# Transposing the second gate-gradient pair and the last filter group by transfers instead of TensorE

## The chip, the core and the metric

One program on one core of a Trainium2 chip. The core has TensorE (matmuls, weight loads), VectorE, ScalarE and GpSimd, a sequencer SP that issues most transfers, and 16 DMA engines that carry them. The metric is device time in microseconds: the median over executions, each compared with executions of the kernel before on the same chip.

## The reference

Forward and backward of one block. `q`, `k`, `v` are 2048 x 512 (sequence by channels); the filter `ssm_k` is 512 x 2048.

```
xn   = layernorm(q)
kv   = (causal 4-tap filter of k with shift_k) * v
y    = causal convolution of kv with ssm_k along the sequence, per channel + kv * ssm_D
s    = xn * y
z    = (sigmoid(xn @ w_gate) * (xn @ w_up)) @ w_down
out  = q + s * silu(z)
```

It returns `out` and the gradients, for a given `grad_out`, of q, k, v, shift_k, ssm_k, ssm_D, w_gate, w_up, w_down. In the backward pass the gradient of `z` (`dz`, 2048 x 512, the "gate gradient" here) is multiplied by the transposed `w_down`, and what comes of it by the transposed `w_gate` and `w_up`.

## The kernel before, in words

The sequence is cut into 16 tiles of 128 rows, taken as 8 pairs (`NP = 8`); the channels into four groups of 128 (`NG = 4`). Convolutions are FFTs of 4096 points, done as matmuls: `step1` multiplies 128x128 tables `Cf` with the 16 column blocks of a group, a 32x32 stream transpose on VectorE follows (`flip`), then `step2`, 32 small matmuls of 32x32 weights in two pairs of PSUM banks. `inv2` and `inv1` go back.

Streams that run side by side: `strG` computes the gated unit pair by pair (`gu_gen`: gate and up matmuls with 256 columns; `z_gen`: 11 matmuls with 512 columns for each tile). `strK` transforms the filter group by group: it loads `KT`, 128 channels x 2048 taps, transposes it into `KC` (16 blocks of 128x128, where block j takes every sixteenth tap), and does `step1` and `step2`. `strV` does the same for `kv`, `strX` multiplies the spectra. Then the backward pass: `zs_gen` computes `dz` of a pair and its transpose `dzT`, `dh_gen` multiplies it by `WdT` (44 matmuls of 256 columns for a pair), `x_gen` multiplies by `WgT` and `WuT` (11 matmuls of 512 columns with each, for each tile). At the end the weights' gradients (`dW`) and the convolution's backward (`frontC`, `backC`).

The pairs go backward in the order `ORD = [5, 6, 7, 4, 3, 2, 1, 0]`, so pair 6 is the second of this order. Of the 8 transposes `dzT` in the kernel before, those of the first two pairs are done by TensorE (8 transposes of 128x128 for a pair, with two copies out of PSUM), the other six by a transposing transfer from SBUF to SBUF. Of the four filter groups all are transposed by TensorE, 16 transposes and two copies of 1,024 columns each.

Nothing is issued in program order. The program is recorded as a list of numbered operations, and `ORDER` gives, written out, the order of the numbers for each engine: `tensor`, `vector`, `scalar`, `gpsimd`, `sync` (SP's transfers); `moves` orders the transfers among each other as the program is emitted. "25 15+1" means 25, 15, 16. Engines take their lists strictly in order. A copy out of PSUM (`evac`) may stand in the list of ScalarE or of VectorE. `BANKS` gives each PSUM tile its place. Every operation is recorded at one line of code (507), so rows of the trace are told apart by tiles, shapes and times; with 4,907 numbers in the tensor list and 4,907 matmuls in the trace, a number's place in time can be counted off.

Numbers that the prediction touches, as the kernel before has them: 3 is the load of columns 0 to 255 of `w_up` on ScalarE's queue, 119 and 127 start the gate and the up matmuls that use those columns for pair 0; 192 is a sigmoid. 1156 to 1163 and 1201 to 1208 are the transposes of the last filter group, 1164 and 1209 their copies, 1360 starts the `step1` matmuls of that group. 1095 is the copy of a `step1` tile of `strV`, 1014 and 1022 a `step2` of `strK`, 1165 to 1174 ten `z_gen` matmuls. 2351 to 2360 are the transposes and copies of pair 6; 2476 and 2482 the transposing loads of `w_gate` and `w_up` into `WgT` and `WuT`, 2265 a small load for `WuT`'s last 96 columns, 2297 a store of `out`; 2474 a load of `grad_out`. 2575 and 2546 start the two tiles of `x_gen` of the first pair, 2586 and 2557 their parts that use `WuT`; 2607, 2627, 2647 and 2655 are `dh_gen` of pair 6.

Of the kernel before, what the change touches and what calls it, by code (L numbers as in the profile page):

```python
# [9 lines left out]
ALU = mybir.AluOpType  # L10
# [13 lines left out]
NJ = 16  # L24
# [53 lines left out]
    """,  # L78
    "vector": """
# [552 lines left out]
def kernel_impl(ctx, tc, A_q, A_k, A_v, A_shift_k, A_ssm_k, A_ssm_D, B_x, B_w_gate, B_w_up, B_w_down,  # L632
# [24 lines left out]
    def ps(kind, shape, dt=f32):  # L657
        return nc.ps(kind, shape, dt)
# [870 lines left out]
```

## Time and profile before

| | before |
|---|---|
| median of 3 runs | 448.35 us (447.02 to 449.74) |
| the profiled execution | 445.85 us, span of the core 443.7 us |
| TensorE matmuls | 435.5 us, 98% of the span, 4,907 |
| TensorE weight loads | 303.8 us, 68% |
| VectorE | 409.3 us, 92%, 629 instructions |
| ScalarE | 279.8 us, 63%, 352 instructions |
| GpSimd | 20.9 us, 5% |
| transfers | 116.85 MB, mean 263 GB/s |

The span runs from the core's first instruction to its last; the profiled execution's own time lies 2.15 us above it. Shares are averages over stages; a matmul's end is modelled. PE is TensorE, PEld its weight loads, DVE VectorE, ACT ScalarE, SP the sequencer that issues transfers; a q behind the name (SPq, ACTq) is that engine's queue. "x16 | 1.2, 227" in a group means 16 instructions, 1.2 us busy together, 227 ns for one.

### The profile page before, as it was taken

Reading aid. Unit: us, or ns where it says so; the run is one execution under the profiler, and the core shown is the slowest. Engines: PE = TensorE matmul, PEld = TensorE weight load, DVE = VectorE, ACT = ScalarE, POOL = GpSimd, SP = SyncE. Lnnn points to the kernel's source line nnn. Section 1 sums busy time; section 2 is a strip of 40 time slices with the busy share of each in tenths; the row PEclk is TensorE's granted clock in tenths of the full one; section 3 lists DMA queues with packets and bytes.
Section 4 is the critical chain, followed back from the end, with each engine's and each line's share of the span. In section 5 each row is a group of like instructions: output and inputs, shape, how many; then the busy total and the mean of one; then the engine's idle time right before and its main releaser. Section 6 shows DMA issues by size and latency. Waiting matters only on the chain.

```text
span 443.7 us, 11573 instructions
## 1 busy us (share of the span) xinstructions
PE 435.5 (98%) x4907; PEld 303.8 (68%) x4907; DVE 409.3 (92%) x629; ACT 279.8 (63%) x352; POOL 20.9 (5%) x46
## 2 busy tenths in 40 slices
PE   7999999999999999999999999999999999999996
PEld 3886686767758678565656654444478888887885
DVE  8999899989988999999999987699889999999993
ACT  6998898888756688545283543534577745574422
POOL 8210110000000000000000000000000000000000
PEclk9999999999999999999999999999999999999999
DMA  7999998678398899999989999999999999999998
GB/s 245 297 349 282 294 315 264 167 273 305 116 312 261 247 222 222 284 322 308 363 236 324 289 216 282 279 241 186 281 258 215 267 267 219 231 249 262 266 258 260
DMA packets 196069, 116.85 MB, mean 263 GB/s; under 512 B 107386, under 2 KB 182706, under 8 KB 195890
## 3 DMA queue, kind: packets, MB, share of 16 engines
q1 hardware_dynamic: 186864, 111.49, 94.5%
q10 hardware_dynamic: 9154, 4.62, 3.5%
q8 instruction: 38, 0.62, 0.6%
q14 instruction: 13, 0.11, 0.1%
HBM read 43.87 MB, written 46.70 MB: 204 GB/s over the span
## 4 chain that ended last, share of the span: by engine, by line
PE 88%; DVE 6%; ACT 2%; DMA 1%; POOL 1%; issue 1%
PE psum L507 88%; DVE slab L507 6%; ACT slab L507 2%; POOL slab L507 1%; DMA slab<-in_A_q_dram 1%; DMA slab<-in_A_ssm_k_dram 1%
## 5 line engine op out<-in xcount | busy, mean ns | idle before, releaser
L507 PE MATMUL psum<-slab 128*128 128x256 bf16 (+5 forms) x4907 | 435.5, 299 | 4.0 <-DVE slab L507 3.2
L507 PEld LDWEIGHTS <-slab 128*128 128x128 bf16 (+2 forms) x4907 | 303.8, 96 | 135.6 <-issue 28.9
L507 ACT CAST slab<-psum 128x1024 bf16<-128x1024 f32 (+5 forms) x224 | 190.4, 892 | 119.5 <-PE psum L507 96.0
L507 DVE TENSOR_TENSOR slab<-slab 128x1024 bf16<-128x1024 bf16 (+4 forms) x302 | 240.2, 830 | 8.0 <-ACT slab L507 6.2
L507 ACT ACTIVATE slab<-slab 128x512 bf16<-128x512 bf16 (+5 forms) x61 | 50.9, 875 | 30.8 <-DVE slab L507 30.7
L507 DVE STREAM_TRANSPOSE slab<-slab 128x1024 f32<-128x1024 f32 x48 | 64.8, 1354 | 1.8 <-ACT slab L507 1.3
L507 DVE CAST slab<-psum 128x1024 bf16<-128x1024 f32 (+3 forms) x29 | 32.6, 1131 | 5.1 <-PE psum L507 4.3
L507 DVE TENSOR_TENSOR slab<-psum,slab 128x512 bf16<-128x512 f32 (+2 forms) x52 | 31.5, 609 | 5.9 <-ACT slab L507 3.8
L507 ACT ACTIVATE slab<-psum 128x512 bf16<-128x512 f32 (+1 forms) x48 | 27.6, 576 | 7.1 <-PE psum L507 6.8
L507 POOL MEMSET slab<- 128x128 bf16 (+3 forms) x10 | 4.5, 448 | 261.8 <-DVE slab L507 149.6
L507 POOL TENSOR_TENSOR slab<-slab 128x2 f32<-128x2 f32 (+3 forms) x11 | 11.0, 1000 | 97.3 <-DVE slab L507 97.2
L507 DVE SCALAR_TENSOR_TENSOR slab<-slab 128x2 f32<-128x2 f32 (+2 forms) x41 | 14.1, 359 | 1.5 <-POOL slab L507 1.2
L507 ACT ACT_TABLE_LOAD x10 | 12.8, 1283 | 1.9 <-issue 1.8
L507 DVE SCALAR_TENSOR_TENSOR slab<-psum,slab 128x512 bf16<-128x512 f32 x16 | 10.7, 684 | 1.9 <-PE psum L507 1.8
L507 DVE BATCH_NORM_STATS2 slab<-slab 128x6 f32<-128x512 bf16 x16 | 10.7, 678 | 1.0 <-DMA slab<-in_A_q_dram 1.0
L507 DVE STREAM_SHUFFLE slab<-slab 128x1024 f32<-128x1024 f32 x8 | 10.5, 1319 | 0.0
L507 ACT COPY slab<-psum 128x1024 bf16<-128x1024 bf16 (+2 forms) x9 | 7.4, 831 | 0.8 <-PE psum L507 0.8
L507 DVE TENSOR_SCALAR slab<-slab 128x512 bf16<-128x512 bf16 (+6 forms) x28 | 7.5, 284 | 0.2
L507 DVE COPY slab<-psum 128x512 bf16<-128x512 bf16 (+1 forms) x10 | 4.7, 492 | 0.1
L507 POOL TENSOR_SCALAR slab<-slab 128x1 f32<-128x1 f32 (+3 forms) x10 | 3.3, 335 | 0.4
L507 DVE MEMSET slab<- 32x192 uint32 (+3 forms) x10 | 1.6, 160 | 1.7 <-PEq L1513 0.9
L507 DVE BATCH_NORM_AGGREGATE slab<-slab 128x2 f32<-128x6 f32 x16 | 2.6, 167 | 0.1
(13 smaller groups left out, 8.4 us busy)
## 6 DMA issues: line engine op xcount, KB each, us to landing
slab<-KD SPq DMA_DIRECT2D x16, 512.0 KB, 5.3
hD<-slab SPq DMA_DIRECT2D x8, 704.0 KB, 6.1
duD<-slab SPq DMA_DIRECT2D x8, 704.0 KB, 5.4
dgD<-slab SPq DMA_DIRECT2D x8, 704.0 KB, 5.1
slab<-in_A_k_dram SPq DMA_DIRECT2D x4, 1024.0 KB, 7.6
KD<-slab SPq DMA_DIRECT2D x8, 512.0 KB, 5.5
VD<-slab SPq DMA_DIRECT2D x8, 512.0 KB, 5.5
out_dram<-slab SPq DMA_DIRECT2D x16, 256.0 KB, 4.1
```

The costliest lines, as they stand in the source:

```text
L507: getattr(getattr(self.nc, eng), meth)(*[place(v) for v in a], **{x: place(v) for x, v in k.items()})
```

## The change

Two transposes move from TensorE to transposing transfers on SP's queue.

In `strK`, the last group (`cg == 3`) no longer uses TensorE: `KT` is copied into `Q` with its taps reordered, so that block j is contiguous (one copy of 128x2048, which `ORDER` gives to ScalarE), and a transposing transfer writes `KC` from `Q`. 16 transposes and two copies of 1,024 columns go.

In `zs_gen`, TensorE transposes only the first pair of `ORD`; the second pair gets a transposing transfer as the later pairs have. 8 transposes and two copies of 512 columns go.

All lists of `ORDER` and `BANKS` are new. The program has 25 operations fewer, so numbers shift: below 1156 they stay; the copy into `Q` is 1156, the transposing transfer to `KC` 1193; from 1210 on a number falls by 16, the transfer of `dzT` of pair 6 is 2335, and from 2361 on a number falls by 25. So 2476 becomes 2451, 2482 becomes 2457, 2265 becomes 2249, 2297 becomes 2281, 2474 becomes 2449, and 2575, 2607, 2546, 2627 become 2550, 2582, 2521, 2602. Twenty copies out of PSUM change from VectorE to ScalarE and 21 from ScalarE to VectorE.

The diff, of `ORDER` only the lines that hold these places:

```diff
...
     "tensor": """
...
-        1210+15 968+7 1042+3 1033+7 1054+1 1087+7 1165+3 1004+7 1169+5 1022+7 1014+7 1056+8 1175 1106+7 1098+7 1238+15
...
-        2443+3 2277+3 2458+1 2272+3 2466+6 2460 2488+15 2351+3 2508+15 2356+3 2536+3 2528+7 2483+3 2627+15 2477+3
-        2607+15 2575+9 2546+10 2655+3 2647+7 2557+10 2702+3 2585+11 2746+15 2706+3 2766+15 2665+7 2794+3 2786+7
...
+        1087+7 1004+7 1157+9 1022+7 1014+7 1054+1 1167 1056+8 1106+7 1098+7 1230+7 1222+7 1287+7 753+7 769+7 745+7
...
+        2401+7 2393+7 2210+15 2418+3 2414+3 2157+15 2425+5 2437+3 2256+3 2261+3 2431+4 2441+6 2463+15 2483+15 2511+3
+        2503+7 2452+3 2550+3 2582+15 2458+3 2521+7 2602+15 2630+3 2622+7 2554+17 2529+13 2677+3 2721+15 2741+15 2769+3
...
     "scalar": """
-        1 68 60+1 66 65 67 249+1 69 327 251+1 307 3 279 112 62 192 410 438 541 363 362 586 596 560 135 477 524 686 385
...
+        1 68 60+1 65+2 249+1 327 69 307 251+1 279 112 62 192 3 410 438 541 363 362 586 560 596 135 524 477 686 220 384
...
+        674 985 966 1002 652+1 1041 976 1210 1050 1156 1095 1312 1030+1 1168 1065 1114+1 1238 778 1303 777 1342 1188+1
...
     "sync": """
...
-        1939 1936 1933 1759 1935 1942 1938 2062 1940 1934 1943 1963 2082 2019 2262 2267 2263 2298 2474 2265 2268 2323
-        2476 2297 2482 2738 2438 2324 2544 2701 2475 2545 2449 2737 1770 2743 2663 2606 1937 2739 2605 2664 2802 2868
...
+        365 937 386 709 506 708 722 655 675 938 617 399 936 707 1193 940 780 1066 793 743 917 1052 1154 1314 1410 1169
...
+        1925 1920 1743 1923 1767 1917 2046 1926 1922 2047 1924 1927 1947 1919 2066 2003 2246 2282 2251 2307 2252 2247
+        2451 2335 2281 2249 2457 2308 2449 2520 2676 2713 2413 2424 2712 2519 2450 2581 2718 2639 2638 2714 2580 1754
...
@@ -977,17 +977,23 @@
             if cg > 0:
                 nc.vector.tensor_tensor(KT[:, 0:1], KT[:, 0:1], Dcol_b[:, cg:cg + 1], ALU.add)
             KC = KC_r.next()
-            for jh in range(2):
-                pt = ps("tr", [8, 128], bf16)
-                for jj in range(8):
-                    nc.tensor.transpose(pt[:, jj, :], KT[:, 8 * jh + jj:S:16], ident)
-                nc.evac(KC[:, 8 * jh:8 * jh + 8, :], pt[:], 1024)
-                if cg == jh == 0:
-                    nc.vector.tensor_tensor(KC[0:1, 0, :], KC[0:1, 0, :], skb[0:1, 0, 0:GW], ALU.add)
+            Q, Qw = QK_r.next()
+            if cg < 3:
+                for jh in range(2):
+                    pt = ps("tr", [8, 128], bf16)
+                    for jj in range(8):
+                        nc.tensor.transpose(pt[:, jj, :], KT[:, 8 * jh + jj:S:16], ident)
+                    nc.evac(KC[:, 8 * jh:8 * jh + 8, :], pt[:], 1024)
+                    if cg == jh == 0:
+                        nc.vector.tensor_tensor(KC[0:1, 0, :], KC[0:1, 0, :], skb[0:1, 0, 0:GW], ALU.add)
+                    yield 1024
+            else:
+                nc.evac(Q[:, 0:S].rearrange("c (j p) -> c j p", j=NJ), KT.rearrange("c (p j) -> c j p", j=NJ), S)
+                yield 1024
+                nc.sync.dma_start_transpose(KC, Q[:, 0:S])
                 yield 1024
             if cg + 1 < NG:
                 ld_KT(cg + 1)
-            Q, Qw = QK_r.next()
             yield from step1(lambda j: KC[:, j, :], Q)
...
@@ -1144,7 +1150,7 @@
         nc.vector.tensor_tensor(a, go, s, ALU.mult)
         nc.vector.tensor_tensor(z, a, z, ALU.mult)
         dzT = T[p]["dzT"] = dzT_r.next()
-        if p in ORD[:2]:
+        if p in ORD[:1]:
             for u in range(2):
                 pt = ps("tr", [4, 128], bf16)
                 for db in range(4):
...
```

## Rows read from the trace of the kernel before

**Rows 1.** Page: engine shares of the span, granted clock in 40 slices

```profile
PE 435.5 (98%) x4907; PEld 303.8 (68%) x4907; DVE 409.3 (92%) x629; ACT 279.8 (63%) x352; POOL 20.9 (5%) x46
...
PEclk9999999999999999999999999999999999999999
```

**Rows 2.** Chain of waits in order of time: start us, us, what

```profile
52.95 330.12 PE psum L507 x3506
```

**Rows 3.** Groups by form, TensorE, 200 to 225 us

```profile
L507 PE MATMUL psum<-slab 128*128 128x512 bf16 x73 | 16.4, 379 | 0.0
L507 PE MATMUL psum<-slab 128*128 128x256 bf16 x88 | 10.1, 273 | 0.0
```

**Rows 4.** Groups by form, TensorE, 175 to 200 us

```profile
L507 PE MATMUL psum<-slab 128*128 128x512 bf16 x81 | 18.3, 379 | 0.0
L507 PE MATMUL psum<-slab 128*128 128x256 bf16 x71 | 8.6, 273 | 0.0
```

**Rows 5.** Groups by form, TensorE, 59.04 to 60.05 us

```profile
L507 PE MATMUL psum<-slab 128*128 128x128 bf16 x16 | 1.2, 227 | 0.0
```

**Rows 6.** Groups by form, TensorE, 168.95 to 171.25 us

```profile
L507 PE MATMUL psum<-slab 128*128 128x128 bf16 x8 | 0.8, 219 | 0.0
```

**Rows 7.** Groups by form, whole span: copies and operations of ScalarE

```profile
L507 ACT ACTIVATE slab<-slab 128x1024 bf16<-128x1024 bf16 x16 | 16.7, 1057 | 0.9 <-DVE slab L507 0.8
...
L507 ACT COPY slab<-psum 128x1024 bf16<-128x1024 bf16 x5 | 5.1, 1035 | 0.3 <-PE psum L507 0.3
```

**Rows 8.** Timeline of SP's queue, 20 to 185 us: start us, us of issuing

```profile
27.21 12.75 SPq L507 DMA_TRANSPOSE slab<-slab  x1
...
70.66 0.36 SPq L507 DMA_DIRECT2D VD<-slab  x1
75.29 0.32 SPq L507 DMA_DIRECT2D zD<-slab  x1
...
119.01 1.28 SPq L507 DMA_TRANSPOSE slab<-slab  x1
...
161.89 8.29 SPq L507 DMA_TRANSPOSE slab<-in_B_w_gate_dram  x1
...
170.90 5.98 SPq L507 DMA_TRANSPOSE slab<-in_B_w_up_dram  x1
...
181.44 1.81 SPq L507 DMA_TRANSPOSE slab<-slab  x1
```

**Rows 9.** Transfers by tensors: count, KB each, median us from issue to landing

```profile
slab<-in_grad_out_dram SPq DMA_DIRECT2D x8, 256.0 KB, 4.5
...
slab<-in_B_w_up_dram ACTq DMA_DIRECT2D x1, 256.0 KB, 8.3
slab<-slab SPq DMA_TRANSPOSE x13, 3.2
...
slab<-in_B_w_gate_dram SPq DMA_TRANSPOSE x1, 10.3
slab<-in_B_w_up_dram SPq DMA_TRANSPOSE x1, 8.1
```

**Rows 10.** Groups by form, TensorE, 82.96 to 83.5 us

```profile
L507 PE MATMUL psum<-slab 128*128 128x128 bf16 x8 | 0.6, 219 | 0.0
```

**Rows 11.** Groups by form, TensorE, 176.45 to 180.9 us

```profile
L507 PE MATMUL psum<-slab 128*128 128x512 bf16 x21 | 4.7, 379 | 0.0
```

**Rows 12.** Groups by form, TensorE, 182.30 to 184.4 us

```profile
L507 PE MATMUL psum<-slab 128*128 128x512 bf16 x11 | 2.5, 379 | 0.0
```

**Rows 13.** Timeline of ScalarE and its queue, 12 to 75 us

```profile
13.92 0.37 ACTq L507 DMA_DIRECT2D slab<-in_B_w_up_dram  x1
...
20.62 0.60 ACT L507 ACTIVATE slab<-psum 128x512 bf16<-128x512 f32 x1
```

**Rows 14.** Groups by form, TensorE, 26.12 to 26.98 us

```profile
L507 PE MATMUL psum<-slab 128*128 128x256 bf16 x8 | 1.0, 273 | 0.0
```

More of the change, by code (lines that the diff above doesn't have):

```diff
@@ L33 @@
     "tensor": """
[44 rows of a table removed]
[45 rows of a table added]
     """,
     "vector": """
[25 rows of a table removed]
[25 rows of a table added]
     """,
     "scalar": """
[17 rows of a table removed]
[16 rows of a table added]
     """,
     "gpsimd": """
-        56 87 57 90 29+1 63 38 34 91 86 98 88 99 115 89 100 116 101 103+2 108 81 109 107 142 106 92 110 102 227 117
-        501 1326 935 912 1657 1929 2261 3541 4743
+        87 57 56 29 88 30 63 90 38 34 115 98+2 92 89 86 101 103+1 91 105 107 106 108 116 109 142 102 110 81 227 117
+        501 935 1310 912 1641 1913 2245 3516 4718
     """,
     "sync": """
[10 rows of a table removed]
[10 rows of a table added]
     """,
     "moves": """
[12 rows of a table removed]
[12 rows of a table added]
     """,
@@ L156 @@
 BANKS = (
-    "32200102131110310001321010100010000101110000101000011101011001001001231011100001100001013101011002011011001001"
-    "00001110101131110101010100100101010001100110101001101001100131032103101012300101121012010131101201011210023110"
-    "01011322211212100102101010310101001123110230110002122120220021301110200311310221010102102013011101120331210301"
-    "21031001012112201301213"
+    "00230121200131030010121010100010000101110000101000011101011001001001110011100001110001013101011020101100101100"
+    "00111010110111010101010010010101001100011010130110100010113103211010123221011310120101311002310131001300102001"
+    "13222112121001021010103101000011021102301100022211202200203011002013113102210101021020130111000202311103012103"
+    "1001111102002301230"
 )
```

202 rows, old and new, of the table ORDER are left out of this document.

## The prediction

> **What bounds the kernel now.** I read the engine shares first: TensorE's matmuls cover 98% of the span, VectorE 92%, the weight loads 68%, and the granted clock is full (the 2.4 GHz level) in every slice [rows 1]. Matmul ends in such a page are modelled, so 98% alone proves little. Next, the chain of waits: one piece of 3,506 matmuls runs for 330 us without a break, from 53 to 383 us [rows 2]; nothing else releases anything in it. Then I tested whether those matmuls are dense. Between 200 and 225 us there are 73 matmuls of 512 columns and 88 of 256 [rows 3]. If 512 costs twice 256, that is 234 units in 25 us, 106.8 ns for 256 columns. Between 175 and 200 us there are 81 and 71, 233 units, 107.3 ns [rows 4]. A different mix gives the same pace, so the engine takes columns without gaps, and I take 107 ns for 256 and 214 ns for 512. In this stretch a matmul removed is time removed, and a matmul that waits is time lost, whatever VectorE does. So the sum below has two sides: TensorE work that goes, and places where the new lists make TensorE wait.
>
> **What is removed.** Sixteen transposes of the filter's last channel group run in one packet at 59.04 us: their busy time is 1.2 us, and one lasts 227 ns, so they start (1.2 - 0.227)/15 = 65 ns apart; sixteen are 1.04 us [rows 5]. Eight transposes of the second pair run as two packets of four, 0.8 us busy together: (0.8 - 2 x 0.219)/6 = 60 ns apart, 0.48 us [rows 6]. Together 1.52 us of TensorE, both inside the unbroken piece.
>
> Each side engine loses copies too: ScalarE two PSUM copies of 1,024 columns (1.04 us each [rows 7]) and one of 512, VectorE one of 512. Neither engine is in the unbroken piece, so this counts as nothing; if VectorE were the path there, it would be a gain of about half a 1,024-column copy, 0.5 us.
>
> A rule of the Trainium skill speaks against the swap: "VectorE: DVE Perf Modes", section "The three transpose paths", has 390 ns for a 128x128 transpose on TensorE and 1,309 ns by transfer. By it (an estimate) 24 transposes would return 9.4 us, not 1.52; the spacing of 60 to 65 ns [rows 5, 6] contradicts that, and the rows decide.
>
> **What is added for the filter group.** First a copy of 128x2048 that reorders the row, placed on ScalarE (the new scalar list has it between a sigmoid and the evacuation of a first-step tile of stream V). The trace has no such form. Lower bound: the two copies it replaces, 2.07 us; a 128x1024 operation SBUF to SBUF is 1.06 us, twice that 2.1 [rows 7]. Upper bound, for its stride of 16 elements, twice as much, 4.2 us. I take 2.1. Behind it in ScalarE's queue stands that evacuation, and the next second-step tiles of stream K need both pairs of banks. Between them TensorE has ten 512-column matmuls, 2.1 us. So the copy costs TensorE between nothing and 2.1 us (4.2 - 2.1); with the middle value the two are level, and I put 0.2 us.
>
> Then a transposing transfer of 128x2048. Nearest rows: 1,024 columns take 1.28 us of issuing, 1.81 where SP is crowded; 4,096 columns 12.75 us [rows 8]. So 2.6 to 6.4 us of SP's queue, landing 3.2 us or more after issue starts [rows 9]. It can start near 72 us, when the copy ends. SP issues nothing from 71.0 to 75.3 us [rows 8], and the first matmul that reads the group comes at 82.96 [rows 10]. Earliest landing near 75, latest near 81: hidden, nothing. Behind it SP holds a store of the shifted keys, a swapped filter load and spills; the spill of 75.29 us can be late by 3 us without anyone waiting soon. Without that hole in SP's time the group would be wanted up to 2 us before it lands, and TensorE would wait as long.
>
> **What is added for the second pair.** One transposing transfer of 128x1024: 1.3 to 1.8 us of SP, 3.2 us to land [rows 8, 9]. It stands between the transposing loads of the gate weight and the up weight, and this is the costly place. Before, SP issues the gate weight from 161.89 for 8.29 us and the up weight from 170.90 for 5.98 [rows 8]; they land 10.3 and 8.1 us after their issue starts [rows 9], at 172.2 and 179.0. First use is at 176.45 and 182.30 [rows 11, 12], slack 4.2 and 3.3 us. The new lists eat this slack from both sides. TensorE's list puts four output matmuls straight after the first pair's 44, ahead of the 32 of the second pair (32 x 107 ns = 3.4 us), so with 1.5 us saved the gate weight is wanted near 176.45 - 1.5 - 3.4 = 171.5. SP's list drops two loads from in front of it, 1.0 to 1.7 us earlier: landing 170.5 to 171.2. The up weight gets the new transfer and a small load ahead of it, 1.7 to 2.2 us more, less the earlier start: landing 179.0 to 180.2, wanted near 182.30 - 1.5 - 0.4 = 180.4. The transfer itself is issued near 169, its input ready by 168.95 where TensorE took it before [rows 6]; it lands near 172.2 and is wanted near 172.3. Three arrivals are just in time. Each costs nothing if its estimate holds, and up to 0.8 us if it is off by a microsecond, as the two issue times of such transfers differ by half of that; I put 0.3 us for all.
>
> **The new order elsewhere.** Most of it permutes matmuls that are dense either way: nothing, since no row shows a gap in there to close or open. One move has a price: the load of the first two up-weight blocks on ScalarE's queue. Before, it is issued at 13.92 us; the new list puts it behind the sigmoid that starts at 20.62 [rows 13], and it took 8.3 us to land [rows 9]. From about 20.6 that is 28.9, while the block is used at 26.12 [rows 14], and the new list turns the two halves so that the up weight comes first. Loads of the same size land in 4.5 us as a median [rows 9]: 25.1, in time. So nothing to 2.8 us; I take 0.3, since in the old place a transfer of many tiny pieces stood just ahead on that queue.
>
> **Sum.** 1.52 - 0.2 - 0.3 - 0.3 = 0.7 us less. The profiled execution took 445.85 us (span 443.7); it becomes 445.1. The runs' median is 448.35, 2.5 us above it, so I forecast 447.6 us. The runs spread over 2.7 us; 0.5%, 2.24 us, is what this measurement can tell from no change.
>
> **Rivals.**
> 1. The first up-weight load is late (slower). It decides from a landing after 26.1 us on; at the full 8.3 us TensorE waits 2.8 us, so 448.35 - 1.5 + 2.8 + 0.5 for the other two places = 450.1. For it: the only row of this load. Against: the tiny pieces ahead of it then. Chance 0.2.
> 2. SP's queue around the two weights (slower). If the new transfer is issued at the pace of the 4,096-column row, 3.2 us, it lands 1.9 us later than wanted and the up weight after it more than a microsecond late, 2 to 3 us together: 448.35 - 1.5 + 2.5 = 449.3. Against: the slack that the earlier start gives. Chance 0.1.
> 3. TensorE isn't the bound, and its work is hidden: 448.35. For it: the weight loads show 68%, a third idle [rows 1]. Against: the equal pace in rows 3 and 4. "Perfetto Trace Analysis", section "Identifying the Most-Contended Engine", of the Trainium skill says to judge TensorE by its weight loads' share, not by matmul time; by it a third of the engine would be free. Chance 0.07.
> 4. The whole gain plus a better start: all three waits at nothing and the opening, before the unbroken piece of rows 2 begins, shorter by 1 to 2 us: 448.35 - 1.5 - 1.5 = 445.3. Nothing in the rows prices it; chance 0.13.
>
> **Numbers.** The forecast case keeps 0.5; alone it reaches from 445.5 to 449.5 (its waits at nothing or at 1.5, and 1.2 us for the medians). The range over all cases reaches to rival 4 below and rival 1 above, with the same allowance: 444.6 to 451.0. Faster by over 0.5% (below 446.1): about 0.22 of the forecast case and most of rival 4, 0.25. Slower (above 450.6): half of rivals 1 and 2 and a little of the rest, 0.21. The rest 0.54.
>
> **What would show it.** TensorE with 24 fewer matmuls and about 1.5 us less busy; a ScalarE copy of 128x2048 near 70 us, at 2.1 us; transposing transfers from slab to slab 15 instead of 13. Idle time or stretched pieces before the first up-weight blocks near 26 us, before the second step near 70 us, and near 171, 172 and 180 us would show the three waits, each with its own releaser. The prediction is wrong if TensorE's gaps grow elsewhere (an order that stalls on banks or on VectorE), or if the span falls by more than the matmuls that went.

## The result, and the profile after

The changed kernel takes 449.18 us, median of 18 executions (446.97 to 452.75), the kernel before 447.55 in the same measurement (445.56 to 449.74): a ratio of 1.0040, 95% interval [1.0022, 1.0058]. By the medians that is 1.6 us slower, where the forecast was a gain of 0.7. The ratio is estimated from all executions and isn't the quotient of the two medians; by it the loss is 1.8 us, between 1.0 and 2.6.

The page of the changed kernel, span, shares and TensorE's clock (rows 1 show these of before):

```profile
span 447.1 us, 11486 instructions
...
PE 434.1 (97%) x4850; PEld 302.9 (68%) x4883; DVE 412.1 (92%) x629; ACT 277.6 (62%) x347; POOL 22.1 (5%) x46
...
PEclk9999999999999999999999999999999999999999
```

The weight loads count what TensorE does: 4,883, 24 fewer, as the change says (33 records of matmuls are missing from this trace). The busy time fell by 1.4 us and the span still grew by 3.4, from 443.7 to 447.1. About 1.4 us of this growth is a stretch at the lower clock in the first 13 us, which not every execution has (last section). For the rest, look at what ended TensorE's waits, first in the kernel before, then in the changed one (engine, what it waited for: us, times, longest):

```profile
PE psum L507 <- DVE slab L507: 3.2, 5, 1.3
PE psum L507 <- DMA slab<-in_A_ssm_k_dram: 0.4, 1, 0.4
```

```profile
PE psum L507 <- DVE slab L507: 4.5, 4, 2.0
PE psum L507 <- ACT slab L507: 1.9, 1, 1.9
PE psum L507 <- issue: 1.6, 3, 1.2
```

The waits grew from 3.6 to 8.0 us, by 4.4 us, which is three times what was saved. Where they lie is read from TensorE's timeline, whose pieces end at a wait (start, length, first matmul of the piece, count, in brackets the idle time ahead of it and its releaser):

```profile
8.66 33.37 PE L507 MATMUL psum<-slab 128*128 128x128 bf16 x379 [1.98 <-DVE slab L507]
...
66.39 6.30 PE L507 MATMUL psum<-slab 128*128 128x128 bf16 x61 [0.63 <-DVE slab L507]
74.56 245.80 PE L507 MATMUL psum<-slab 32*32 32x512 bf16 x2191 [1.86 <-ACT slab L507]
...
429.20 14.70 PE L507 MATMUL psum<-slab 128*128 128x256 bf16 x186 [1.24 <-issue]
```

The unbroken piece of before [rows 2] is broken at 66 and at 72.7 us, and there is a new hole at 428. The last two are new and large, 3.1 us together. What ScalarE did at 72.7 us:

```profile
68.91 0.89 ACT L507 ACTIVATE slab<-psum 128x512 bf16<-128x512 f32 x2
69.66 3.93 ACT L507 COPY slab<-slab 128x2048 bf16<-128x2048 bf16 x1
73.46 1.05 ACT L507 CAST slab<-psum 128x1024 bf16<-128x1024 f32 x1
```

The copy of the filter's last group takes 3.93 us, not 2.1, and the eviction behind it (73.46) is what TensorE's second step waits for. That is the place which the prediction named, at nine times its price. On SP's queue around the two weights, which the prediction feared as well, everything comes in time:

```profile
164.42 5.29 SPq L507 DMA_TRANSPOSE slab<-in_B_w_gate_dram  x1
171.11 1.23 SPq L507 DMA_TRANSPOSE slab<-slab  x1
172.39 0.57 SPq L507 DMA_DIRECT2D out_dram<-slab  x1
173.02 0.43 SPq L507 DMA_DIRECT2D slab<-in_B_w_up_dram  x1
173.49 5.70 SPq L507 DMA_TRANSPOSE slab<-in_B_w_up_dram  x1
```

Issuing the gate weight took 5.3 us instead of 8.3 [rows 8]; it landed at 173.3 and was first used at 175.8, the up weight at 181.3 and 185.0. TensorE's matmuls show no wait between 74.6 and 320 us. Its weight loads do stop once in this place, at the first matmul of `x_gen`, and what they wait for is VectorE and not the gate weight:

```profile
175.85 0.76 PEld L507 LDWEIGHTS <-slab 128*128 128x128 bf16 x5 [0.25 <-DVE slab L507]
```

Experiment 8 shows what this stop costs.

### The profile page after: what moved, and what is told of

It is laid out like the page before. It is cut to its first block, busy times and chain, and to the rows that moved or that the text cites. A ratio compares the mean times of both kernels' runs of the same rounds, so it can differ in the third digit from the quotient of the medians.

```text
span 447.1 us, 11486 instructions
## 1 busy us (share of the span) xinstructions
PE 434.1 (97%) x4850; PEld 302.9 (68%) x4883; DVE 412.1 (92%) x629; ACT 277.6 (62%) x347; POOL 22.1 (5%) x46
## 4 chain that ended last, share of the span: by engine, by line
PE 77%; DVE 16%; issue 4%; ACT 2%; POOL 1%; DVEq 0%; ACTq 0%; POOLq 0%
PE psum L507 77%; DVE slab L507 16%; ACT slab L507 2%; POOL slab L507 1%; DVEq L507 0%; ACTq L507 0%; POOLq L507 0%; POOLq L1519 0%
## 5 line engine op out<-in xcount | busy, mean ns | idle before, releaser
L507 ACT CAST slab<-psum 128x1024 bf16<-128x1024 f32 (+4 forms) x221 | 188.1, 895 | 134.3 <-PE psum L507 94.0
L507 ACT ACTIVATE slab<-slab 128x512 bf16<-128x512 bf16 (+5 forms) x62 | 52.3, 876 | 20.1 <-DVE slab L507 20.0
L507 DVE CAST slab<-psum 128x1024 bf16<-128x1024 f32 (+4 forms) x32 | 35.5, 1118 | 10.2 <-PE psum L507 9.8
L507 POOL TENSOR_TENSOR slab<-slab 128x2 f32<-128x2 f32 (+3 forms) x11 | 12.5, 1143 | 95.4 <-DVE slab L507 95.3
L507 DVE TENSOR_SCALAR slab<-slab 128x512 bf16<-128x512 bf16 (+6 forms) x27 | 8.7, 337 | 1.2 <-POOL slab L507 1.0
L507 ACT COPY slab<-psum 128x1024 bf16<-128x1024 bf16 (+2 forms) x7 | 5.5, 833 | 1.2 <-PE psum L507 1.2
L507 DVE COPY slab<-psum 128x512 bf16<-128x512 bf16 (+1 forms) x8 | 3.8, 481 | 1.2 <-PE psum L507 1.2
L507 ACT COPY slab<-slab 128x2048 bf16<-128x2048 bf16 x1 | 3.9, 3932 | 0.0
```

The source lines that it names most:

```text
L507: getattr(getattr(self.nc, eng), meth)(*[place(v) for v in a], **{x: place(v) for x, v in k.items()})
```

## The experiments

Each was timed against the kernel before on the chip it ran on; the ratios are to that kernel. Its median was 448.50 us beside experiments 1, 2, 4 and 5, 448.89 beside 3, 6 and 7, 448.06 beside 8 and 9, and 447.43 beside 10 and 11. A ratio and the quotient of two medians differ by up to 0.3% here, so differences of a microsecond are read from the traces, where the times of one order repeat far better (within 0.04 us up to 424 us in the two profiles of the changed kernel).

**1. The copy behind the eviction that it held up.** In ScalarE's list:

```diff
-... 1210 1050 1156 1095 1312 ...
+... 1210 1050 1095 1156 1312 ...
```

> The changed kernel with one move: ScalarE's 128x2048 copy of the filter's last group stands behind the eviction that it held up, not ahead of it. Theory 1 (the copy took 3.93 us where the prediction put 2.1, and TensorE waited 1.86 us behind it): TensorE's wait of 1.86 us at 72.7 us goes, the copy's transfer lands about 1 us later and still ahead of its first reader, and the time falls by 1.2 to 1.9 us against the changed kernel (449.18), to 447.3 to 448.0, a ratio to the kernel before of 0.999 to 1.001. Theory 2 (the wait only moves: the next evictions stand behind the same copy and TensorE stops at the next banks): a wait of over 1 us stays between 72 and 82 us, and the ratio stays at 1.003 to 1.006. Theory 3 (the loss lies in the first 13 us of the new order, where TensorE stood idle 2 us and then ran at the lower clock): the wait goes, but the time falls by under 0.5 us.

Measured: 448.72 us, ratio 1.0012 [0.9988, 1.0036]. TensorE's wait is still there, 3.1 us of work later (the piece ahead of it has 9.36 us instead of 6.30):

```profile
65.06 9.36 PE L505 MATMUL psum<-slab 128*128 128x128 bf16 x89 [0.63 <-DVE slab L505]
76.28 242.96 PE L505 MATMUL psum<-slab 32*32 32x512 bf16 x2163 [1.86 <-ACT slab L505]
```

By the trace theory 2 holds: the wait moved to the next evictions, at the same 1.86 us. The ratio lies between the two theories' ranges and tells little by itself.

**2. The copy without its regrouping.**

```diff
-nc.evac(Q[:, 0:S].rearrange("c (j p) -> c j p", j=NJ), KT.rearrange("c (p j) -> c j p", j=NJ), S)
+nc.evac(Q[:, 0:S], KT, S)
```

> The changed kernel with the 128x2048 copy reading its source in order instead of with a step of 16 elements; the last filter group then goes through the transposing transfer without its regrouping. It stands where it stood. Theory 1 (the step in the source doubles the copy's time, and the price is a matter of size alone): the copy takes 2.0 to 2.2 us, twice the 1.04 us of a 128x1024 copy of the kernel before, TensorE's wait at 72.7 us falls from 1.86 to under 0.3 us, ratio 0.998 to 1.001. Theory 2 (a copy of 2048 columns between two places of the on-chip memory takes 3.9 us however it reads): the copy stays at 3.9 us and the ratio at 1.003 to 1.006.

Measured: 446.84 us, ratio 0.998 [0.9961, 1.0000]. The copy, and TensorE around it:

```profile
68.30 1.92 ACT L507 COPY slab<-slab 128x2048 bf16<-128x2048 bf16 x1
```

```profile
65.03 252.02 PE L507 MATMUL psum<-slab 128*128 128x128 bf16 x2252 [0.63 <-DVE slab L507]
```

The copy takes 1.92 us without the step in its read, a little under the 2.0 to 2.2 of theory 1, and TensorE has no break until 317 us. Theory 1 holds: for a copy of this size the step doubles the time.

**3. The step on the write side.** The same data arrive, read in order and written with a step of 128 elements.

```diff
-nc.evac(Q[:, 0:S].rearrange("c (j p) -> c j p", j=NJ), KT.rearrange("c (p j) -> c j p", j=NJ), S)
+nc.evac(Q[:, 0:S].rearrange("c (j p) -> c p j", j=NJ), KT.rearrange("c (p j) -> c p j", j=NJ), S)
```

> The changed kernel with the copy's regrouping moved from the read to the write: ScalarE reads the filter's 2048 columns in order and writes them with a step of 128, at the same place in its list, and the data that arrive are the same. Theory 1 (the step in the read is what costs): the copy takes 1.9 to 2.1 us as the copy without regrouping did (1.92), TensorE's wait at 72.7 us is gone, ratio 0.997 to 1.000. Rival (any step costs, on whichever side): the copy stays at 3.9 us, TensorE waits 1.8 us, ratio 1.003 to 1.005.

Measured: 456.33 us, ratio 1.0188 [1.0155, 1.0221]. Both expectations missed: the copy got far longer.

```profile
68.31 9.32 ACT L507 COPY slab<-slab 128x2048 bf16<-128x2048 bf16 x1
```

```profile
78.53 247.70 PE L507 MATMUL psum<-slab 32*32 32x512 bf16 x2191 [7.19 <-ACT slab L507]
```

As a dose it serves well. A copy of 1.92 us costs TensorE no wait, 3.93 costs 1.86, 9.32 costs 7.19: the copy's time less 2.1 us (2.07, 2.13), which is the cover of ten 512-column matmuls in the prediction. The formula was right; the value put into it was wrong. The kernel's time grew by somewhat more than the wait; TensorE's granted clock stood at 0.50, the level of 1.2 GHz, from 76 to 82 us, in the end of the wait and behind it.

**4. The copy on GpSimd**, ahead of its next small operation (912).

```diff
-nc.evac(Q..., KT..., S)
+nc.add([("gpsimd", "tensor_copy", (Q..., KT...), {})])
 scalar:
-1156
 gpsimd:  ... 1310
+1156
          912 ...
```

> The changed kernel with the 128x2048 copy on GpSimd, which is busy 22 of 447 us, ahead of its next small operation. Theory 1: TensorE's wait of 1.86 us goes, since ScalarE evicts at once; ratio 0.998 to 1.001 if GpSimd needs at most 8 us for the copy (the transfer is issued at 73.6 us now and its first reader comes at 86.2). If the copy slows VectorE beside it, VectorE's operations between 70 and 78 us get longer than in the changed kernel (1.21 us for a 128x1024 cast), and up to 1 us of the gain is lost. Rival: GpSimd takes over 8 us, the transfer lands late, and TensorE waits for it before 86 us: ratio over 1.004.

Measured: 448.71 us, ratio 0.9991 [0.9968, 1.0015]. The 1.86 us became two short waits of TensorE, 0.28 and 0.39, as theory 1 expected. GpSimd needs the same time as ScalarE, and one small VectorE operation beside it takes longer and ends with it (TensorE, GpSimd, VectorE):

```profile
73.92 2.33 PE L505 MATMUL psum<-slab 128*128 128x512 bf16 x10 [0.28 <-DVE slab L505]
76.64 10.04 PE L505 MATMUL psum<-slab 32*32 32x512 bf16 x144 [0.39 <-ACT slab L505]
```

```profile
69.59 3.92 POOL L505 COPY slab<-slab 128x2048 bf16<-128x2048 bf16 x1 [0.51 <-ACT slab L505]
```

```profile
72.11 1.43 DVE L505 TENSOR_SCALAR slab<-slab 128x2 f32<-128x2 f32 x1
```

In the changed kernel that operation, at 72.07 us, took 0.16.

**5. Both parts in the old order.** The lists and banks of before, renumbered, without the 24 transposes; the changed kernel's code.

```diff
 scalar:  ... 1095 1050 1012
+1156
          1031 1030 ...
 sync:    ... 936 938
+1193
          940 675 ... 2451
+2335
          2281 2457 ...
```

> Both parts of the change in the order of the kernel before: its lists and banks as they were, without the 24 transposes, with the copy on ScalarE between the second and the third of the evictions around it, the transposing transfers at the same neighbours on SP's queue as in the changed kernel. It tells the two parts from the new order. Theory 1 (the two parts gain what leaves TensorE, 1.5 us, less a late copy; the loss was the place of the copy and the new order's start): ratio 0.996 to 0.999, TensorE's first 20 us as in the kernel before, with the full clock. Rival (the transposing transfers cost what they save, through the queue or through the data's late arrival): a wait of about 1 us at the first reader of the last filter group near 82 us or near 172 us, ratio 1.000 to 1.004.

Measured: 453.19 us, ratio 1.0087 [1.0051, 1.0123]. TensorE's waits, the new ones of its timeline:

```profile
75.97 0.41 PE L504 MATMUL psum<-slab 32*32 32x512 bf16 x8 [1.94 <-ACT slab L504]
76.88 58.69 PE L504 MATMUL psum<-slab 32*32 32x512 bf16 x740 [0.51 <-ACT slab L504]
...
175.90 112.14 PE L504 MATMUL psum<-slab 128*128 128x256 bf16 x700 [1.06 <-DMA slab<-slab]
...
430.11 16.98 PE L504 MATMUL psum<-slab 128*128 128x256 bf16 x246 [2.64 <-DMA slab<-duD]
```

Theory 1 fails. The rival's mechanism shows at one of its two places, 1.06 us at the first reader of the second pair's transfer (the first reader of the filter group waits for nothing), and its ratio was too mild. Two more waits stand beside it: 2.45 us behind the copy and 2.64 at a transposing load late in SP's queue. Together they are 6.15 us, less 1.5 saved 4.65. The medians differ by 4.69, but by the ratio it is 3.9 us (2.3 to 5.5), so the close match is luck. The new order as a whole shows no loss: put into the old order at these places, the two parts cost about twice as much by the ratios (3.9 us against 1.8; the two intervals just overlap). Why the load at 430 us came so late wasn't followed up.

**6. The start of before.** The old lists for all that starts in the first 30 us, then the changed kernel's.

```diff
 tensor:
-25 15 7+7 157+7 22 49+3 167+7 ...
+25 15+1 7+7 157+7 167+7 44+3 49+3 ... (282 numbers of before, then what is left of the list)
```

> The changed kernel with the lists of the kernel before for all that the engines start in the first 30 us (and the banks of those tiles), then its own order; the copy is as in the changed kernel. Theory 3 (part of the loss is in the new start: TensorE's largest wait there was 1.98 us at 6.7 us against 1.25 in the kernel before, and 3.3 us at the lower clock followed in the profiled execution): the granted clock is 1.00 in all of the first 20 us, TensorE is 0.8 to 2.3 us further at 30 us, ratio 1.000 to 1.002. Rival: the new start was only a rearrangement, and what it loses before 20 us it had given back by 60 us (0.65 us between 30 and 40 and 0.54 between 50 and 60): ratio 1.003 to 1.005.

Measured: 449.29 us, ratio 1.0019 [0.9994, 1.0044]. The time decides between neither. In the trace the wait at the start is 1.17 us instead of 1.98, but one of 0.96 opens at 34.7 us, where the two orders were joined:

```profile
35.62 4.95 PE L505 MATMUL psum<-slab 32*32 32x512 bf16 x70 [0.96 <-DVE slab L505]
64.93 6.30 PE L505 MATMUL psum<-slab 128*128 128x128 bf16 x61 [0.63 <-DVE slab L505]
73.10 247.47 PE L505 MATMUL psum<-slab 32*32 32x512 bf16 x2191 [1.86 <-ACT slab L505]
```

TensorE begins the piece behind the 0.63 us wait at 64.93 us; the executions of the new start whose clock stayed full begin it at 65.03 to 65.07. So this old start gives back 0.1 us, and what the joint took from it can't be told apart. The wait of 1.86 us behind the copy is unchanged.

**7. The run of short matmuls cut up.** In TensorE's list:

```diff
-... 5927 5814+63 5972+1 5978+1 6009 5980+1 5928 6010 5740 5929+1 5935+1 5982+4 5937+6 ...
+... 5927 5814+15 (8 of the following) 5830+15 (8) 5846+15 (8) 5862+15 ...
```

> The changed kernel with the 64 short matmuls (32 rows out, 128 columns) at 426.2 us cut in four groups of 16, eight of the 256-column matmuls that follow them between each two. TensorE stands idle for 1.24 to 1.55 us right behind that run in all four kernels with the new order, and no semaphore and no transfer ends it. Theory 4 (its instructions ran out: they came in blocks 200 matmuls apart there, against some 130 on average, and the run of short matmuls eats them up faster than they come): the idle time falls under 0.4 us and the time by about 1 us, ratio 1.000 to 1.003. Rival (something else holds TensorE there, a transfer or an engine that the profile doesn't name): the same matmul still starts 1.2 to 1.5 us late.

Measured: 448.44 us, ratio 1.0021 [0.9997, 1.0046]. The ratio is inside the theory's range, but its interval excludes neither no change nor the changed kernel's 1.0040; the trace decides. The hole is gone, and TensorE's last piece begins at 422 us and runs to the end:

```profile
422.10 20.61 PE L505 MATMUL psum<-slab 128*32 128x128 bf16 x340 [0.21 <-ACT slab L505]
```

**8. The second pair on TensorE again, in the new order.**

```diff
-        if p in ORD[:1]:
+        if p in ORD[:2]:
 tensor:
+(4 transposes) ahead of 2483, (4) behind 2498
```

> The changed kernel with the second pair's gate gradients turned by eight TensorE transposes and two evictions again, as in the kernel before, in the new order; the filter group is as in the changed kernel. Theory (in the new order the transferred pair is hidden: its transfer is issued at 171.1 us and its first reader comes at 176.7, behind no wait): TensorE's work between 170 and 180 us grows by 0.5 us and nothing else changes there, so the time grows by about 0.5 us, ratio 1.004 to 1.006. Rival (the transfer holds up the two weight loads beside it on SP's queue, and so costs what it saves): the weight load behind it is issued over 1 us earlier than in the changed kernel and the ratio is at or below 1.004, the changed kernel's own.

Measured: 451.06 us, ratio 1.0062 [1.0037, 1.0086], just above the theory's range. The up weight's transposing load is issued 3.7 us earlier than in the changed kernel (1.3 of it because the changed kernel's profile lost time to the lower clock), as the rival said, but the ratio isn't at or below 1.004, so the transfer does not cost what it saves.

The two executions can be laid beside each other by the count of weight loads; ahead of the first transpose this kernel is 0.04 us behind that of experiment 7. Its eight transposes add 0.45 us; the prediction counted 0.48. At the first matmul of `x_gen` 0.25 us of this goes again: the stop of the weight loads behind VectorE, shown above for the changed kernel, isn't there:

```profile
173.75 1.73 PEld L505 LDWEIGHTS <-slab 128*128 128x128 bf16 x15
```

So moving the second pair gave TensorE 0.2 us and not 0.48: without the transposes it came to that place before VectorE's result. The rest of the growth is the hole at 428 us:

```profile
428.59 15.42 PE L505 MATMUL psum<-slab 128*32 128x128 bf16 x194 [2.01 <-issue]
```

This kernel also tells what that hole hangs on. All matmuls behind 175 us stand 8 places later in the list. If the hole belonged to a matmul, it would come 8 weight loads later; if it belongs to the stream of instructions, it stays at the same count. The first row is the changed kernel from 0 to 428.5 us, then this kernel from 0 to 428 us; both windows end inside the hole (length, PE busy and its records, PEld and its records, ...):

```profile
0.00:428.50 428.50, 419.37 (x4664) 289.76 (x4697) 400.97 (x606) 272.43 (x338) 22.12 (x46) 1.00 1.02 263
```

```profile
0.00:428.00 428.00, 418.49 (x4664) 289.26 (x4697) 401.73 (x608) 273.23 (x339) 22.17 (x46) 1.00 1.01 262
```

There are 4,697 weight loads in both, and as many ahead of the hole in experiments 1 to 4 and 11 (4,698 in experiment 6). The hole sits at a place in TensorE's instruction stream. Instructions come over a queue of their own, from the page of the changed kernel:

```profile
q8 instruction: 38, 0.62, 0.6%
```

These are 38 packets of 16 KB for TensorE's 9,766 loads and matmuls, one for 128 pairs on average. In the changed kernel three of the last ones start at 416.0, 426.7 and 432.1 us, 200 and 56 pairs apart. In all eight profiles with the hole, of seven kernels, TensorE goes on 2.3 to 2.5 us after the second of these packets starts; in experiments 7, 9 and 10, with the run cut up, it comes to the same place 2.7 to 2.9 us after it and finds no hole. That TensorE starves there is shown by the place, by this distance and by experiment 7. A run of 64 short matmuls alone doesn't do it: the kernel before has four such runs, at 335, 380, 419 and 426 us, and no hole behind any. Its last two lie 124 weight loads apart, each between two packets of its own. In the changed kernel they lie 85 apart, and the first and most of the second fall between the packets at 416.0 and 426.7 us. Why that packet came no sooner isn't shown.

**9. Both mendings together,** the copy on GpSimd and the run cut up.

```diff
+nc.add([("gpsimd", "tensor_copy", (Q..., KT...), {})])
 tensor:
+... 5927 5814+15 (8 of the following) 5830+15 ...
```

> The changed kernel with the copy on GpSimd and the run of 64 short matmuls cut in groups of 16: the two mendings that each took away one wait, together. Theory (the loss of the changed kernel is the wait behind the copy, 1.86 us, and the idle time behind the run of short matmuls, 1.24 to 1.55 us, and the two are independent): TensorE's wait at 72.7 us is under 0.7 us as with the copy on GpSimd alone, the idle time at 428 us under 0.4, the time 2 to 2.5 us below the changed kernel's, ratio to the kernel before 0.996 to 0.999, which beats both kernels. Rival (the end is set elsewhere, so that what is taken away in one place is waited for later): ratio 1.000 to 1.003 though both waits are gone.

Measured: 447.36 us, ratio 0.9986 [0.9966, 1.0006]. Both waits are gone as each was alone (0.30 and 0.39 us are left of the first). The ratio is inside the theory's range, but the interval doesn't exclude that nothing was gained.

**10. The copy halved between ScalarE and GpSimd,** and the run cut up.

```diff
-nc.evac(Q..., KT..., S)
+Qj, Kj = Q[:, 0:S].rearrange("c (j p) -> c j p", j=NJ), KT.rearrange("c (p j) -> c j p", j=NJ)
+nc.evac(Qj[:, 0:8, :], Kj[:, 0:8, :], S)
+nc.add([("gpsimd", "tensor_copy", (Qj[:, 8:16, :], Kj[:, 8:16, :]), {})])
```

> The changed kernel with the copy halved, 1024 columns on ScalarE at the old place and 1024 on GpSimd at the same time, and the run of 64 short matmuls cut in groups of 16. Theory (TensorE's wait is the copy's time on ScalarE less the 2.1 us that ten 512-column matmuls cover: 1.86 for 3.93, 7.19 for 9.32, none for 1.92): each half takes 1.95 to 2.0 us, no wait is left at 72.7 us, the transfer is issued 2 us earlier, VectorE is free of GpSimd by 71.6 us, and the ratio to the kernel before is 0.995 to 0.998. Rival (the halves slow each other, or the loss lies in the rest of the new order): a wait of over 0.5 us stays there, or the ratio stays at 0.998 to 1.002.

Measured: 445.95 us against 447.43, ratio 0.9973 [0.9953, 0.9994]: as the theory expected, a little faster than the kernel before and 3.1 us faster than the changed kernel (experiment 11, on the same chip). The halves on ScalarE and on GpSimd, and TensorE:

```profile
68.31 2.08 ACT L505 COPY slab<-slab 128x1024 bf16<-128x1024 bf16 x1
```

```profile
68.21 2.05 POOL L505 COPY slab<-slab 128x1024 bf16<-128x1024 bf16 x1 [0.51 <-ACT slab L505]
```

```profile
65.05 354.86 PE L505 MATMUL psum<-slab 128*128 128x128 bf16 x3881 [0.63 <-DVE slab L505]
420.12 20.33 PE L505 MATMUL psum<-slab 128*32 128x128 bf16 x340 [0.21 <-ACT slab L505]
```

2.08 us is a little over the 1.95 to 2.0 expected but within the cover of 2.1, and TensorE's matmuls run from 65 to 420 us without a break. One expectation was missed: the transfer isn't issued 2 us earlier but at 73.1 us, since SP's queue was busy with a store until 73.0. No matmul waited for it.

**11. The changed kernel again,** beside experiment 10.

> The changed kernel itself once more, on the chip of the kernel above, so that the two are compared directly and that the two waits of its first profile are seen in a second execution: 1.86 us behind the copy and 1.2 to 1.6 us behind the run of short matmuls, ratio 1.002 to 1.006. Rival (the second wait belonged to single executions): it is under 0.5 us here.

Measured: 449.06 us, ratio 1.0043 [1.0022, 1.0064]. Both waits come again at the same places:

```profile
74.58 340.70 PE L507 MATMUL psum<-slab 32*32 32x512 bf16 x3712 [1.87 <-ACT slab L507]
...
429.25 14.70 PE L507 MATMUL psum<-slab 128*128 128x256 bf16 x186 [1.25 <-issue]
```

## Why the prediction was wrong

The forecast was wrong in sign: -0.7 us forecast, +1.6 measured. The frame held, one term was mis-sized and one loss had no term.

- **TensorE bounds the kernel:** right. Of the copy's three times, what exceeds 2.1 us shows in TensorE's wait, and the kernel's time follows in the same direction. Rival 3 is out. The rule that stood beside it, "Perfetto Trace Analysis", section "Identifying the Most-Contended Engine", of the Trainium skill, judges TensorE by the rate of its arithmetic and by the share of its weight loads. By the second of these, 68%, a third of the engine would be free; the measurement decides against it here, since the 1.86 and 7.19 us of wait did not hide in that third.
- **1.52 us removed:** the count was right, the gain smaller. With both waits mended 1.2 us of it arrive (0.9973 [0.9953, 0.9994] of 447.43). Of the second pair's 0.48 us the traces of experiment 8 show 0.2 arriving, since 0.25 became a stop behind VectorE. Its time can't show as little: the interval is over four times 0.48 us wide. The filter group's 1.04 us were not measured alone.
- **The copy: this is the step that failed.** The prediction had the right wait, the right cover (2.1 us) and the bounds 2.07 to 4.2, took 2.1 for the copy and 0.2 us for the wait. Measured 3.93 and 1.86. The nearest rows [rows 7] were of operations that read in order; the one thing in which this copy differs, a step of 16 elements (32 bytes) in its read, was known, stood in the upper bound, and was priced at nothing in the value taken. Read in order the same copy takes 1.92. "SBUF — State Buffer", section "Door 1: The DMA port swizzle (why `[64,N]` ≈ `[32,N]`)", of the Trainium skill says that the on-chip memory has lines of 16 bytes, and that an access which goes to a new line pays for it. A step of 32 bytes is always a new line, and the traces agree with 3.93 against 1.92, though no run tried other steps in the read to show that the line is the reason. The page gives no price; for a write with a step 9.32 us is the only row.
- **The transfer to KC hidden:** right. It was issued at 73.6 us, landed at 81.8, and was first read at 86.2.
- **The second pair between the weights, 0.3 us:** no transfer was waited for in the new order. The size came out near, 0.25 us, by another mechanism, VectorE's late result, so this match is luck. The first reader of the pair came at 176.7 us where the prediction had 172.3, but 3.2 us of this is TensorE's own lateness, from the lower clock and the copy: in experiment 10, which has neither, it comes at 173.5, and no transfer is waited for there either. In the old order the pair's transfer costs 1.06 us (experiment 5): data that arrive late in this place are a real price, which the new order avoids. Rival 2's slow issuing was not seen (1.23 us).
- **The first up-weight load, 0.3 us, and rival 1:** 0. The load is issued at 21.7 us and landed at 24.4, and its first reader comes at 28.6, not 26.1, since the start was rearranged as well. No wait lies there.
- **The new order elsewhere, "nothing":** wrong in one place for certain. The hole of 1.24 us at 428 us, 1.25 in a second execution, is the term the sum lacked. It is in no row of before, and the sum had no way to it; this is the second step that failed. Smaller terms can't be read from the two traces: in the changed kernel the start waits 0.6 us longer (1.63 and 1.98 against 1.27, 0.45 and 1.25) and 0.63 come in at 66 us, but the profiled execution of before lies 1.7 us under its own median, more than these terms.

Put together: -1.5 + 1.86 + 1.25 + 0.25 = +1.9 us, against 1.8 (1.0 to 2.6) by the ratio and 1.6 by the medians. That the two waits are there and can be taken away is shown in the traces, singly (experiments 2, 4 and 7) and together (9 and 10). By time it is clear for the copy, since the whole interval of experiment 2 lies below the changed kernel's, and for both together, 3.1 us between experiments 10 and 11, as large as their sum. For the hole alone the time shows nothing. What is left to the rest of the new order follows from experiment 10: -1.2 us measured of -1.5, so 0.3 us, with an interval of 0.9 to either side. The stop of 0.25 us behind VectorE is of that size and is in that kernel too; that it is all of the rest isn't shown, and what the new start costs stays open.

## What to carry to other kernels

When work moves from the bounding engine to another, the price isn't the moved work but what stands behind it in the new engine's list: write down the cover (here 2.1 us) and ask how sure the duration is against just that number. A row with the same shape but another access pattern is not a row for the operation; where the bounds straddle the cover, take the pattern's side or halve the operation over two engines. And when work leaves the bounding engine, ask which engine it will then wait for: here 0.25 of 0.48 us went to VectorE. After a reordering, look at long runs of very short matmuls as at a resource of their own, above all where two stand close together: they use up instructions faster than any row of busy time shows.

## What was not expected of the hardware

- **The step decides a copy's time.** 128x2048 in bf16 on ScalarE: 1.92 us in order, 3.93 with a step of 32 bytes in the read, 9.32 with a step of 256 bytes in the write. GpSimd needs 3.92 for the second form, the same as ScalarE; the two halves beside each other take 2.08 and 2.05 us.
- **TensorE can run out of instructions.** "Runtime: NRT & Kernel Launch", section "Instruction fetch mechanics", of the Trainium skill has blocks of 16 KiB, 256 instructions, fetched ahead over the engine's own queue and mostly hidden. The sizes agree with the page (38 packets, 0.62 MB). Hidden they are not behind two runs of 64 matmuls of 128 columns and 32 rows that lie 85 weight loads apart: TensorE is idle for 1.09 to 2.01 us at weight load 4,697, in seven kernels. Behind the other runs of this kind they are.
- **The clock after a short idle time.** In the changed kernel's profile TensorE stood idle 1.98 us up to 8.66 us, and then its granted clock was 0.61 on average over 4.4 us; in experiment 7 it stood idle 2.23 us at the same place and the clock stayed full (the window of the idle time, then the one behind it; the last three numbers are clock, DMA share, GB/s):

```profile
7.00:8.60 1.60, 0.00 (x0) 0.00 (x0) 1.11 (x4) 1.40 (x2) 1.58 (x3) 1.00 1.09 363
8.60:13.00 4.40, 4.34 (x39) 2.40 (x39) 3.19 (x10) 2.32 (x3) 3.90 (x18) 0.61 1.01 334
```

```profile
7.00:8.60 1.60, 0.00 (x0) 0.00 (x0) 1.11 (x4) 1.40 (x2) 1.58 (x3) 1.00 1.08 336
8.60:13.00 4.40, 4.34 (x53) 2.91 (x54) 4.34 (x12) 3.62 (x6) 3.90 (x18) 1.00 1.00 320
```

There are 39 weight loads against 54 in the same 4.4 us; from 10 to 12 us the clock stood at 0.50, the level of 1.2 GHz. What it cost can be read at the piece behind the 0.63 us wait, which begins at 66.39 us there and at 65.03 in experiment 7: 1.36 us. Two of the other nine profiled executions with this start, those of experiments 4 and 11, show the same. A wait in the middle can cost more than its length in the same way: in experiment 6 the clock stood at 0.50 from 74 to 76 us, right behind the 1.86 us wait, and TensorE lost 1.7 us against the changed kernel's profile, whose clock stayed full there. None of this is the cause of the result: in experiment 11 the mean clock of the timed executions is 0.998 for both kernels, and those with 0.999 or more have medians of 448.08 us (changed, 7 executions) and 446.83 (before, 6), 1.25 us apart.
